# Attention and mixture of experts on one core: a table of slots for expert 0 alone, the other experts' slots by matrix products, and POOL's DMAs in the attention released a few at a time

## The chip, the cores and the metric

One Trainium2 chip, one of its cores. The metric is the device time of one execution in microseconds (us), the median over runs. Engines are named as in the profile: PE is TensorE's matmul, PEld its weight load, DVE is VectorE, ACT is ScalarE, POOL is GpSimd, SP is SyncE. POOLq and SPq are the DMAs that POOL and SP issue.

## The reference, cut to what matters

```python
# attention: 8 batches, 8 heads, 576 positions, head size 64; heads 0-3 see a plain window of 32,
# heads 4-7 a window of 128 with every fourth position
scores = np.where(masks, scale * np.matmul(q, k.transpose(0, 1, 3, 2)), -1e9)
attn = softmax(scores)
x = np.matmul(attn, v).transpose(0, 2, 1, 3).reshape(4608, 512)
# mixture of experts: 4608 tokens, 8 experts, two of them for each token
noisy_logits = x @ w_gate + np.log1p(np.exp(x @ w_noise)) * noise
top2 = np.argpartition(-noisy_logits, 2, axis=1)[:, :2]
top2_w = softmax over the two logits
for e in range(8):
    for k in range(2):
        mask = top2[:, k] == e
        h = np.maximum(x[mask] @ w1[e], 0.0)          # 512 -> 1024
        out[mask] += top2_w[mask, k, None] * (h @ w2[e])   # 1024 -> 512
```

## The kernel before, in words

**Attention.** 24 steps (`NS = 6 * U`), each of which treats 384 positions of four heads for a pair of batches. The loop is a pipeline that is written out: in turn i it emits the score products of step i (`qk`, tile `s`, line 337 and 348), the exponential of step i-1 (`expo`), its transposes (`ptr`, tile `pp`), the store and the transposes of step i-2 (`store_x`, `x_transpose`, tile `xtp`), the products with v of step i-1 (`pv`, tiles `o` and `x`, line 388) and the gate's products of step i-2 (`gate_mm`, tile `gp`, line 436). A turn has two slots; `at(kb, f)` hangs a piece of work on a slot. The results go to `xs` in HBM.

**Gate and table.** `gate(t0, n)` is a generator that works on n groups of 128 tokens in small pieces: the logits, the two best experts and their weights, and the place of each token in the list of each expert (a running count by a product with a triangle of ones, tile `posp`). `micro` lets the generators emit a few pieces at a time between the parts of a turn. Each token has two entries; an entry is a row of eight words (four row numbers of `xs`, the weight, the token's number). POOL scatters the entries into a table `tab` in HBM with an indirect DMA for each 128 tokens and each of the two experts (line 577): 72 of them. `room` limits how many of these are emitted in a slot. The table's rows beyond the entries are padding that `setup_c` writes at the start.

**Experts.** For each expert the SP queue reads its part of the table into `ixt` and `ixs` (`idx_dma`), DVE copies it into `ixi` (`idx_copy`), POOL gathers x by these numbers (`gather`, line 716, four indirect DMAs for 128 tokens; expert 0 has its own form, line 710), DVE transposes (`xsplit`, tile `xr`, line 733) and ACT and DVE split into a high and a low part (lines 735 and 736). Expert 0's transposes are PE's (`xrp`, line 730). An expert's up to 1216 tokens make up to 10 tiles in three blocks. `up` forms h for a block in eight parts of 12 products (line 764), ACT and DVE take each part out of PSUM as `hh` and `hl` (lines 768 and 769); `down` forms the output of a tile with 24 products (line 805), DVE scales it by the weight (`y`, line 814) and POOL adds it to the output's rows with an indirect DMA (line 782). The order is (up 0, down 2 of the expert before, up 1, down 0, up 2, down 1); expert 0 starts differently. First block of expert 0: its gathers and transposes fall into the attention's last turns.

**What sets the order.** After the attention `plan(t, f)` puts work into a list by the time t at which PE should be there, counted in PE's columns (`tick`); the engines execute what is emitted for them in that order, each waiting only for what an instruction needs. So a number in a `plan` call says behind which of PE's instructions something stands, not when it runs. In particular POOL had, in the attention, nothing that held its scatters back once their inputs (`si`, `en`) were there, except the scatter's own issue.

Of the kernel before, what the change touches and what calls it, by code (L numbers as in the profile page):

```python
# [9 lines left out]
F32 = mybir.dt.float32  # L10
# [11 lines left out]
T = NB * S  # L22
# [18 lines left out]
US_W2 = 3.0, 3.5  # L41
US_X = (17, 52)
# [3 lines left out]
def attention_moe_kernel(ctx, tc, qt, kp, kd, vpl, vdl, w_gate, w_noise, noise, w1, w2, out, CAPS=(1216, 1216, 1216, 1184, 1184, 1152, 1152, 1152), SPLITS=(0, 384, 896)):  # L46
# [19 lines left out]
    xq = xs.rearrange("r (q d) -> (r q) d", d=128)  # L66
    tab = dram.tile([E * ET, TC], I32, name="tab")

# [4 lines left out]
    ixp = ctx.enter_context(tc.tile_pool(name="ixp", bufs=3))  # L73
# [121 lines left out]
    i8 = gat.tile([128, NG, E], F32, name="i8")  # L195
# [5 lines left out]
    def setup_a():  # L201
# [7 lines left out]
        gpsimd.iota(i8, pattern=[[0, NG], [1, E]], base=0, channel_multiplier=0,  # L209
                    allow_small_or_imprecise_dtypes=True)  # L210
        gpsimd.iota(ebase, pattern=[[ET, E]], base=0, channel_multiplier=0,
                    allow_small_or_imprecise_dtypes=True)
        gpsimd.tensor_copy(base, ebase)
        for e in range(E):
# [4 lines left out]
    def setup_b():  # L219
# [3 lines left out]
        t = tokc[:, :, 5]  # L223
        v, s, i0, r, z, a = (acon.tile([128, 2, NT], I32, name=f"tc{i}") for i in range(6))
        gpsimd.iota(v[:, 0].rearrange("p (s j) -> p s j", j=3), pattern=[[0, 12], [128, 3]], base=0, channel_multiplier=1)
        vector.tensor_scalar(a[:, 0], t, 2, None, op0=OP.bitwise_and)
        vector.tensor_scalar(v[:, 1], t, 2, None, op0=OP.logical_shift_right)
        vector.scalar_tensor_tensor(v[:, 1], a[:, 0], 72.0, v[:, 1], op0=OP.mult, op1=OP.add)
        for u in range(U):
            c = slice(NG * u, NG * u + NG)  # L230
            gpsimd.iota(s[:, 0, c].rearrange("p (s j) -> p s j", j=3), pattern=[[768, 3], [0, 3]],
                        base=768 * (6 * u + 3), channel_multiplier=0)
            vector.tensor_scalar(a[:, 0, c], t[:, c], float(TU * u + S), 144.0, op0=OP.is_ge, op1=OP.mult)
            vector.scalar_tensor_tensor(v[:, 1, c], v[:, 1, c], -288.0 * u, a[:, 0, c], op0=OP.add, op1=OP.add)
            vector.memset(s[:, 1, c], 4608 * u)
# [61 lines left out]
    def micro(n=1):  # L297
# [4 lines left out]
        for g in list(gens):  # L302
            while n > 0 and g not in held:
# [6 lines left out]
                if r == 2:  # L310
                    room[0] -= 1
# [835 lines left out]
```

## Time and profile before

| what | us |
|---|---|
| median of 3 runs (1181.67 to 1186.98) | 1183.1 |
| profiled execution | 1184.15 |
| its span, first to last instruction | 1182.5 |
| PE busy / DVE / ACT / POOL over the span | 1026.8 / 467.6 / 298.9 / 519.9 |
| last product of the gate before the first `up` | 265.1 |
| first `up` product of expert 0 | 265.6 |

The profiled execution took 1.65 us beyond its span. The granted clock of PE was 0.941 over the span. PE carries the time: from 500 us on it is busy for 95 to 100 us of each 100, before that for 59 to 77. The stretches in which it is less busy are therefore what a change can win, and what is added to PE later on is what it can lose.

### The profile page before, as it was taken

The numbers are of one execution on the slowest core, as the hardware profiler recorded it, in microseconds if no ns is written. First come the engines' busy times: TensorE is split into PE (matmuls) and PEld (weight loads), VectorE is DVE, ScalarE is ACT, GpSimd is POOL, SyncE is SP. The second block draws the span as 40 slices with busy tenths as digits, with TensorE's granted clock in tenths as the row PEclk, the third lists the DMA queues.
The fourth block names the chain that finished last, engine by engine and source line by source line (L and its number), as shares of the span: only waits on it lengthen the run. The fifth ranks groups of instructions, "written<-read, shape, count | busy, mean of one in ns | idle before, by whom it ended". The sixth has DMA issues, their size and how long they took to land. (4 is left out here: it accounts for less than half of the span.)

```text
span 1182.5 us, 18050 instructions
## 1 busy us (share of the span) xinstructions
PE 1026.8 (87%) x7278; PEld 865.2 (73%) x7279; DVE 467.6 (40%) x1077; ACT 298.9 (25%) x540; POOL 519.9 (44%) x637
## 2 busy tenths in 40 slices
PE   5885737667589899899999998999999999999996
PEld 3663535446378787788889887978888898878885
DVE  6762524344223335243432433343434334332321
ACT  6442413342111223122222312231222223122210
POOL 5006062526456453745644562465246445624012
PEclk9997879777699999899999998999999999999998
DMA  8794538437033233352434333343424353432223
GB/s 287 266 331 182 206 126 299 150 127 271 11 62 63 70 94 94 63 115 52 118 56 108 83 89 63 81 107 74 106 47 116 68 97 91 84 94 45 54 28 45
DMA packets 70967, 133.71 MB, mean 113 GB/s; under 512 B 29520, under 2 KB 29568, under 8 KB 69600
## 3 DMA queue, kind: packets, MB, share of 16 engines
q1 hardware_dynamic: 48176, 93.22, 23.4%
q0 software_dynamic: 22704, 39.30, 18.6%
q8 instruction: 58, 0.95, 0.3%
q14 instruction: 29, 0.24, 0.1%
HBM read 92.19 MB, written 40.29 MB: 112 GB/s over the span
## 5 line engine op out<-in xcount | busy, mean ns | idle before, releaser
L764 PE MATMUL up<-x,w1h 128*128 128x512 f32 (+4 forms) x1536 | 403.4, 349 | 43.1 <-issue 16.8
L764 PEld LDWEIGHTS up<-x,w1h 128*128 128x128 f32 x1536 | 278.9, 194 | 70.3 <-DVE hl L769 18.8
L716 POOL DMA_INDIRECT g<-xs,ixi x258 | 259.7, 1007 | 107.9 <-issue 84.2
L764 PE MATMUL up<-x,w1l 128*128 128x384 f32 (+4 forms) x768 | 266.3, 347 | 1.7 <-issue 1.6
L782 POOL DMA_INDIRECT out_rows<-y,ixs x67 | 106.3, 1586 | 310.6 <-DVE y L814 260.9
L805 PE MATMUL dn<-w2h,hh 128*128 128x512 f32 x576 | 227.4, 395 | 3.3 <-issue 1.8
L805 PE MATMUL dn<-w2l,hh 128*128 128x512 f32 x576 | 226.1, 393 | 4.4 <-issue 4.4
L805 PE MATMUL dn<-w2h,hl 128*128 128x512 f32 x576 | 225.9, 392 | 3.0 <-issue 3.0
L769 DVE SCALAR_TENSOR_TENSOR hl<-up,hh 128x384 fp32r<-128x384 f32 (+2 forms) x192 | 105.7, 556 | 299.0 <-ACT hh L768 205.9
L768 ACT ACTIVATE hh<-up 128x384 fp32r<-128x384 f32 (+4 forms) x192 | 92.7, 498 | 320.7 <-PE up L764 197.0
L764 PEld LDWEIGHTS up<-x,w1l 128*128 128x128 f32 x768 | 149.1, 194 | 12.2 <-issue 1.8
L805 PEld LDWEIGHTS dn<-w2h,hl 128*128 128x128 f32 x576 | 109.3, 190 | 27.4 <-issue 4.3
L805 PEld LDWEIGHTS dn<-w2h,hh 128*128 128x128 f32 x576 | 109.5, 190 | 26.9 <-issue 4.3
L805 PEld LDWEIGHTS dn<-w2l,hh 128*128 128x128 f32 x576 | 109.5, 190 | 26.6 <-issue 4.7
L577 POOL DMA_INDIRECT tab<-en,si x72 | 70.2, 975 | 115.1 <-DVE den L397 55.5
L814 DVE TENSOR_SCALAR y<-dn,ixs 128x512 f32<-128x512 f32 x63 | 46.9, 748 | 127.8 <-PE dn L805 121.5
L735 ACT CAST x<-xr 128x512 fp32r<-128x512 f32 x67 | 40.5, 605 | 175.8 <-DVE xr L733 144.1
L649 DVE TENSOR_TENSOR w1l<-ws,w1h 128x1024 fp32r<-128x1024 f32 x32 | 38.7, 1218 | 75.3 <-ACT w1h L647 67.7
L388 PE MATMUL o<-vp,pt 128*32 128x130 f32 x576 | 32.1, 296 | 30.3 <-ACT pt L371 16.7
L710 POOL DMA_INDIRECT g<-xs,ixf x40 | 38.3, 958 | 42.8 <-DMA kt<-in_kp 21.7
L647 ACT CAST w1h<-ws 128x1024 fp32r<-128x1024 f32 x32 | 33.1, 1048 | 92.8 <-DMA ws<-in_moe_w 92.8
L733 DVE STREAM_TRANSPOSE xr<-g 128x512 f32<-128x512 f32 x67 | 45.8, 683 | 20.5 <-DMA g<-xs,ixi 16.2
(184 smaller groups left out, 839.4 us busy)
## 6 DMA issues: line engine op xcount, KB each, us to landing
ws<-in_moe_w SPq DMA_DIRECT2D x64, 512.0 KB
out_rows<-zero SPq DMA_DIRECT2D x38, 256.0 KB
vd<-in_vdl SPq DMA_DIRECT2D x24, 390.0 KB
vp<-in_vpl SPq DMA_DIRECT2D x16, 585.0 KB
xs<-x SPq DMA_DIRECT2D x24, 384.0 KB
qt<-in_qt SPq DMA_DIRECT2D x14, 576.0 KB
kt<-in_kd SPq DMA_DIRECT2D x16, 320.0 KB
g<-xs,ixi POOLq DMA_INDIRECT x258
```

Of the source, the lines that this page charges most:

```text
L577: ins = gpsimd.indirect_dma_start(out=tab, out_offset=bass.IndirectOffsetOnAxis(ap=si[:, kq, t:t + 1], axis=0), in_=en[:, kq, t], in_offse ...
L649: return lambda: vector.tensor_tensor(b, s, a.bitcast(F32), op=OP.subtract)
L710: gpsimd.indirect_dma_start(out=g[0:rn, c], out_offset=None, in_=xq[0:rows], in_offset=bass.IndirectOffsetOnAxis(ap=IX[0][0][0:rn, t, c:c ...
L716: gpsimd.indirect_dma_start(out=g[:, j], out_offset=None, in_=xq, in_offset=bass.IndirectOffsetOnAxis(ap=IX[e][1][:, r0 // 32 + j:r0 // 32 ...
L733: vector.transpose(xr[:, :, 0:rn].rearrange("p c (g t) -> p g c t", t=32), g[:, 0:n].rearrange("p g (c d) -> p g c d", d=32))
L735: scalar.copy(xh[:, :, o:o + rn], xr[:, :, 0:rn])
L764: tensor.matmul(p[:, 0:n], lhsT=a[:, 128 * f:128 * f + 128], rhs=b[:, kc, 0:n], start=(i == 0), stop=(i == 11))
L768: scalar.activation(hh[:, f, 0:n], p[:, 0:n], AF.Relu)
L769: vector.scalar_tensor_tensor(hl[:, f, 0:m], p[:, 0:m], 0.0, hh[:, f, 0:m].bitcast(F32), op0=OP.max, op1=OP.subtract)
L782: ins = gpsimd.indirect_dma_start(out=out, out_offset=bass.IndirectOffsetOnAxis(ap=sc[0:rn, t, 1:2], axis=0), in_=y[0:rn], in_offset=None, ...
L805: tensor.matmul(p[0:rn], lhsT=a[:, f, o:o + rn], rhs=b[:, f % 2], start=(i == 0), stop=(i == 23))
L814: vector.tensor_scalar(y[0:rn], p[0:rn], wsc, None, op0=OP.mult)
```

## The change

1. **Only expert 0 has a table.** A token's entry for expert 0 goes into `tab0`; a token that is not expert 0's writes into a row that nobody reads. So there is one scatter for each 128 tokens, 36 instead of 72, and the padding is a table of 10 rows a partition instead of 292.
2. **The other experts' slots come from products.** After all gates, DVE and ACT make for each of the 72 (group of 128 tokens, choice) a matrix A of ones where the slot modulo 128 matches, and a matrix V with the token's number in the column of expert and tile; PE sums A'V over all 72 into `acc` (128 x 70): the token of each slot. DVE then works out from it the output rows (`rw`), the numbers for the gathers (`xi`) and where the weight lies (`wi`). The weights are stored by token and expert in `wtab`; POOL gathers them, one indirect DMA for each tile of experts 1 to 7 (`weights`, 67 in all), after each `up` has begun. `idx_dma` and `idx_copy` for experts 1 to 7 are gone. `BULK` places the pieces: 135 of them every 0.36 us of planned time from 15 us after expert 0's start, the rest at 64 us.
3. **POOL's DMAs in the attention are released by turns.** `pool_turn` stands before each scatter and each gather of expert 0's first block. Once a turn it emits a copy of one element of `x`, the result of the latest `pv`, so that POOL waits for that step; three DMAs may follow (four from slot 40 on), each behind a memset as before.
4. **Later transposes.** `LAG`: the transposes of a gathered tile are planned 15 us behind its gather instead of 7 or 8; expert 1's gathers start at 64.1 us of expert 0 with smaller distances.
5. Smaller moves: the gates of groups 18 to 23 and 24 to 26 are one of nine groups at slot 43; the token numbers are worked out by a generator instead of at once.

```diff
-    def new_slot(scatters, speed=1):
-        room[0], rate[0] = scatters, speed
+    def new_slot(scatters, speed=1):
+        if scatters:
+            room[0], fresh[0] = scatters, True
+        rate[0] = speed
         held.clear()
+    def pool_turn():
+        while room[0] <= 0:
+            yield 1
+        if fresh[0] and not experts[0]:
+            gpsimd.tensor_copy(spacer, late["x"])
+        else:
+            gpsimd.memset(spacer, 0.0)
+        fresh[0] = False
+        room[0] -= 1
...
-        new_slot(*((3, 1) if kb < 28 else (4, 2)))
+        new_slot((0 if kb % 2 else 3 if kb < 40 else 4), 1 if kb < 28 else 2)
...
         for t in range(n):
-            for kq in range(2):
-                gpsimd.memset(spacer, 0.0)
-                ins = gpsimd.indirect_dma_start(
-                    out=tab, out_offset=bass.IndirectOffsetOnAxis(ap=si[:, kq, t:t + 1], axis=0),
-                    in_=en[:, kq, t], in_offset=None)
+            yield from pool_turn()
+            ins = gpsimd.indirect_dma_start(
+                out=tab0, out_offset=bass.IndirectOffsetOnAxis(ap=si[:, t:t + 1], axis=0),
+                in_=en[:, t], in_offset=None)
...
+    def slots():
...
+        for i in range(m + 3):
+            if i < m:
+                if i % 4 == 0:
+                    av = late["stage"].tile([128, 4, 256], F32R, name="av", tag="ws")
+                A, V = av[:, i % 4, 0:128], av[:, i % 4, 128:128 + NO]
+                if i % 2:
+                    vector.tensor_scalar(A, iof, lo[:, i:i + 1], None, op0=OP.is_equal)
+                else:
+                    scalar.activation(A, iof, AF.Abs, bias=nlo[:, i:i + 1])
+                    scalar.activation(A, A.bitcast(F32), AF.Relu, scale=-1.0, bias=one)
+                vector.tensor_scalar(V, iof[:, 0:NO], d[:, i:i + 1], tokf[:, i // 2:i // 2 + 1],
+                                     op0=OP.is_equal, op1=OP.mult)
+                ops[i] = (A, V)
+            if i >= 3:
+                A, V = ops.pop(i - 3)
+                tensor.matmul(acc, lhsT=A, rhs=V, start=(i == 3), stop=(i == m + 2), skip_group_check=True)
+            yield
...
+    def weights(e, t):
+        c, rn = NC * (e - 1) + t, TLS[e][t][1]
+        gpsimd.indirect_dma_start(out=late["wq"][0:rn, c:c + 1], out_offset=None, in_=wtab,
+                                  in_offset=bass.IndirectOffsetOnAxis(ap=late["wi"][0:rn, c:c + 1], axis=0))
...
+    def first_block():
+        for t in range(BLS[0][0][0], BLS[0][0][1]):
+            for c in range(4):
+                yield from pool_turn()
+                gather(0, t, (c,))
+                yield 0
...
+            bulk = others()
+            for i in range(135):
+                plan(start + BULK[0] + BULK[1] * i, lambda: next(bulk, None))
+            plan(start + BULK[2], lambda: [None for _ in bulk])
             experts[0] = True
         else:
-            plan_x(e, 2, start + 2, 7, 8)
+            plan_x(e, 2, start + 2, 7, LAG)
         if not last:
-            t = start + (42 if first else 20)
-            plan(t, lambda e=e: (new_idx(e + 1), idx_dma(e + 1, 0, CAPS[e + 1])))
-            plan(t + 8, lambda e=e: idx_copy(e + 1, 0, CAPS[e + 1]))
-            t = max(t + 9, at_[0, 1])
-            plan_x(e + 1, 0, t, 7, 8)
-            plan_x(e + 1, 1, t + 21, 8, 8)
+            t = max(start + (BULK[2] + 0.1 if first else 29), at_[0, 1])
+            plan_x(e + 1, 0, t, *((5, 10) if first else (7, LAG)))
+            plan_x(e + 1, 1, t + (15 if first else 21), *((5, 12) if first else (7, LAG)))
...
+                if e:
+                    for i, ti in enumerate(range(BLS[e][bi][0], BLS[e][bi][1])):
+                        plan(now[0] + 1 + 1.5 * i, lambda ti=ti, e=e: weights(e, ti))
                 up((e, bi), X.pop((e, bi)), BLS[e][bi][3], tail(e, bi))
```

Three places show how the instructions stand. First POOL in the attention, where the scatters of the first gate begin. `tab` is the table of all experts, `spacer` a tile of one element, `en` and `si` a group's entries and their places. Before:

```order
L281 MEMSET free 128x784
L576 MEMSET spacer 1x1
L577 DMA tab<-en,si 37376x8
L576 MEMSET spacer 1x1
L577 DMA tab<-en,si 37376x8
```

And after, where `tab_58` is the table of expert 0 and `x` the result of the latest step:

```order
L246 IOTA tokc 128x36
L343 COPY spacer<-x 1x1
L640 DMA tab_58<-en,si 9216x8
L345 MEMSET spacer 1x1
L640 DMA tab_58<-en,si 9216x8
L345 MEMSET spacer 1x1
L640 DMA tab_58<-en,si 9216x8
L343 COPY spacer<-x 1x1
L640 DMA tab_58<-en,si 9216x8
```

Before, the pair of memset and scatter repeats 36 times (two gates) with nothing of the attention in between; now each three scatters stand behind a copy from a step's `x`. In the whole attention there are 13 such groups: six of three scatters, the gathers of expert 0's first block as groups of 3, 4, 4 and 1, and the third gate's scatters as 4, 4 and 1. Behind them stand 16 gathers and nine scatters without copies; before, that last stretch was 16 gathers and 12 scatters, and six more scatters later.

The second place is PE at the beginning of expert 0's second `up` (tiles `w1h`, `w1l`: the high and low part of w1; `x`: the split tokens). Before:

```order
L805 MATMUL dn<-w2h_3556,hl 128x512
L764 MATMUL up<-x,w1h_2842 128x512 x2
L764 MATMUL up<-x,w1l_2843 128x512
L764 MATMUL up<-x,w1h_2904 128x512 x2
L764 MATMUL up<-x,w1l_2905 128x512
L764 MATMUL up<-x,w1h_3100 128x512 x2
L764 MATMUL up<-x,w1l_3101 128x512
L764 MATMUL up<-x,w1h_3142 128x512 x2
L764 MATMUL up<-x,w1l_3143 128x512
```

And after, with `acc` the sum over all tokens and `av` the pairs of A and V:

```order
L987 MATMUL dn<-w2h_3487,hl 128x512
L946 MATMUL up<-x,w1h_2715 128x512 x2
L946 MATMUL up<-x,w1l_2716 128x512
L946 MATMUL up<-x,w1h_2791 128x512 x2
L946 MATMUL up<-x,w1l_2792 128x512
L946 MATMUL up<-x,w1h_3029 128x512 x2
L946 MATMUL up<-x,w1l_3030 128x512
L946 MATMUL up<-x,w1h_3058 128x512 x2
L946 MATMUL up<-x,w1l_3059 128x512
L755 MATMUL acc<-av 128x70 x7
```

Behind each of the eight parts of that `up` there now stand seven to nine products into `acc`; the other 12 of the 72 stand in the `down` ahead of it.

The third place is POOL in the middle experts (`ixi`, and `xi` after, hold the numbers for the gathers; `out_rows` is the output). Before:

```order
L782 DMA out_rows<-y,ixs 4864x512
L716 DMA g<-xs,ixi 128x128 x9
L781 MEMSET spacer 1x1
L782 DMA out_rows<-y,ixs 4864x512
L781 MEMSET spacer 1x1
```

And after, with `wq` the weights of the slots:

```order
L964 DMA out_rows<-y,rw 4864x512
L900 DMA wq<-wtab,wi 128x1
L894 DMA g<-xs,xi 128x128 x4
L900 DMA wq<-wtab,wi 128x1 x2
L894 DMA g<-xs,xi 128x128 x5
L963 MEMSET spacer 1x1
L964 DMA out_rows<-y,rw 4864x512
```

The gathers and the output's DMAs are as many as before; nine or ten gathers of weights for each expert stand among them, and no read of a table on SP or DVE is left there.

More of the change, by code (lines that the diff above doesn't have):

```diff
@@ L1004, in attention_moe_kernel, with others @@
             plan(2.0 * (kb - NK - 5), f)
+    def others():
+        while not ready[0]:
+            yield
+        late["en"] = gat.tile([128, 2, 2 * NT], F32, name="lg", bufs=2)
+        late["en2"] = gat.tile([128, 2 * NT], F32, name="lg", bufs=2)
+        yield from slots()
     start = 0.0
```

429 lines of the change are left out of this document (295 added, 134 removed).

## The prediction

> **What bounds the kernel now.** I read the page's slices first, then windows of whole steps, then the two timelines of PE and POOL where a window was poor, and last the windows and rows behind the attention. The slices (29.6 us each) show PE short of work in the first ten and nearly full from the eighteenth on:
>
> ```profile
> PE   5885737667589899899999998999999999999996
> PEclk9997879777699999899999998999999999999998
> ```
>
> The program is thus two parts: an attention that PE could do faster and experts that PE bounds. A step of the attention begins with the same product each time, and these rows give its length when nothing disturbs it:
>
> ```profile
> 45.92 0.50 PE L337 MATMUL s<-mask,identb 128*128 128x512 bf16 x2
> 78.68 0.50 PE L337 MATMUL s<-mask,identb 128*128 128x512 bf16 x2
> ```
>
> Five steps lie between them: (78.68 - 45.92) / 5 = 6.55 us. Cutting at the same product, I find four single steps of four times that length or a little less. The windows below hold those five good steps together, the four long ones, the step behind the first of these, and the stretches up to and behind the attention's end at 265.6 (columns: length, busy time and instructions of PE, PEld, DVE, ACT and POOL, granted clock, DMA share, GB/s):
>
> ```profile
> 45.92:78.68 32.76, 29.26 (x643) 24.12 (x640) 20.19 (x53) 17.04 (x38) 1.07 (x3) 1.00 0.93 352
> 94.44:122.40 27.96, 12.55 (x132) 6.58 (x130) 3.95 (x12) 3.21 (x6) 18.97 (x36) 0.67 0.31 107
> 122.40:131.38 8.98, 8.36 (x131) 6.70 (x130) 3.69 (x9) 3.21 (x6) 0.00 (x0) 0.71 0.72 252
> 153.11:181.89 28.78, 9.70 (x130) 6.97 (x127) 3.94 (x12) 3.75 (x9) 18.75 (x35) 0.65 0.26 91
> 195.24:210.59 15.35, 8.69 (x140) 6.12 (x137) 7.72 (x41) 3.81 (x10) 7.73 (x9) 0.85 1.02 408
> 217.44:243.00 25.56, 12.94 (x136) 6.97 (x131) 7.08 (x30) 6.36 (x15) 16.72 (x28) 0.75 0.25 80
> 265.60:283.00 17.40, 17.34 (x91) 16.86 (x90) 11.25 (x55) 4.52 (x10) 9.64 (x11) 0.85 0.65 217
> 283.00:312.60 29.60, 8.61 (x22) 5.78 (x21) 1.18 (x10) 1.43 (x2) 20.43 (x34) 0.58 0.43 146
> ```
>
> In each long step PE has its usual 130 to 140 instructions, while POOL works nearly without pause. What POOL does there is indirect DMAs back to back: 18 scatters in the first and in the second, 8 gathers in the third, and 12 scatters with 4 gathers in the fourth, 60 in all; 28 more follow at 273.2. First and last of the first burst, a group of six later that stands by itself, and the burst of 28:
>
> ```profile
> 96.30 1.09 POOL L577 DMA_INDIRECT tab<-en,si  x1 [33.63 <-DVE si L572]
> 117.97 0.96 POOL L577 DMA_INDIRECT tab<-en,si  x1 [0.23 <-issue]
> 259.90 0.96 POOL L577 DMA_INDIRECT tab<-en,si  x1 [20.66 <-DVE den L397]
> 266.87 0.96 POOL L577 DMA_INDIRECT tab<-en,si  x1 [0.23 <-issue]
> 273.22 0.98 POOL L710 DMA_INDIRECT g<-xs,ixf  x1 [5.39 <-issue]
> 307.47 0.96 POOL L577 DMA_INDIRECT tab<-en,si  x1 [0.22 <-issue]
> ```
>
> The period is (117.97 - 96.30) / 17 = 1.27 us a DMA, and its last ends at 118.93, 3.5 us before the step does. The mechanism that I read: while POOL issues these, PE's instructions are let through only slowly.
>
> ```profile
> 106.00:122.00 16.00, 4.80 (x16) 1.78 (x17) 0.00 (x0) 0.00 (x0) 10.80 (x22) 0.50 0.03 3
> 112.16 0.37 PE L436 MATMUL gp<-xt,wg 128*32 128x128 f32 x1 [0.85 <-issue]
> 113.57 0.44 PE L436 MATMUL gp<-xt,wg 128*32 128x128 f32 x2 [1.04 <-issue]
> ```
>
> Two products start in 1.41 us, so one instruction per 0.70 us (matmuls or weight loads), each with idle time put to "issue", that is to no semaphore. The DMA share of 0.03 says that the transfers are not what is full. But it doesn't begin at once. From a burst's first DMA until PE falls to that pace, PE still works through some 100 instructions:
>
> ```profile
> 96.30:100.82 4.52, 3.33 (x52) 2.64 (x49) 2.18 (x3) 1.72 (x3) 3.87 (x7) 1.00 0.73 244
> 153.82:157.40 3.58, 2.86 (x59) 2.12 (x47) 0.91 (x2) 1.41 (x4) 3.14 (x6) 1.00 0.97 360
> 198.04:202.96 4.92, 2.58 (x49) 1.96 (x47) 4.43 (x30) 2.11 (x5) 3.85 (x4) 1.00 1.01 409
> 218.91:225.25 6.34, 3.20 (x59) 2.52 (x48) 4.07 (x9) 3.31 (x4) 5.14 (x8) 1.00 0.41 147
> ```
>
> So PE has a store of about 100 instructions (96 to 107), good for 3.6 to 6.3 us, in the mean 4.8; a burst that ends before it is used up should cost nothing.
>
> **The change part by part.** *Pacing and 36 scatters fewer.* The four steps are 27.96 + 28.78 + 15.35 + 25.56 = 97.65 us; four good ones are 26.2, so 71.4 us are lost in them, and another 2.4 in the step of 8.98 us behind the first, which runs at a clock of 0.71. With 13 groups of one to four DMAs, one behind each step's `x`, I let all of it go: -73.8.
>
> *What the groups still cost.* Three DMAs last 3.8 us and four 5.1. Against the mean store of 4.8 us the seven groups of three cost nothing and the four groups of four run over by 0.3 us; once starved, PE recovered late (3.5 us above). From below: 0, since the six scatters from 259.90 on, 7.9 us, left PE busy in 265.60:283.00 for 17.34 of 17.40 us. From above, with the shortest store of 3.6 us and 3.5 us of recovery each: 7 x (3.8 + 3.5 - 3.6) + 4 x (5.1 + 3.5 - 3.6) = 46. I take 2 us for each group of four: +8, near the low end, as three of the four stores seen outlast a group of three.
>
> Each copy waits for `pv` of its turn, and behind it on POOL are only the next scatters and gathers. Of the attention nobody waits for a scatter; expert 0's gathers and the first `up` wait for the table, and their groups are last. The first scatter ran at 96.30, in the thirteenth of 24 steps; with the two turns that drain the pipeline 14 turns are left for the 13 groups, so this just fits, and what is late is within the bounds of the term behind the attention.
>
> *Transfers.* The attention without stalls is denser. A row for its queue up to 265.6:
>
> ```profile
> q1 hardware_dynamic: 15414, 56.70, 58.9%
> ```
>
> 58.9% of 265.6 is 156 us, so an attention of 200 us has a share of 0.78, and the good steps above ran at 0.93. Contention: 0 to 5, I take +2. The padding's smaller writes and the moved gate of nine groups are in there; the smaller work for `en` on DVE is hidden beside a PE that is busy for 29.26 of 32.76 us.
>
> By the Trainium skill (DMA: Bandwidth & Descriptors, "Issuing engines are not separate DMA queues") DMAs of all issuing engines share the same 16 engines, and spreading them saves only the sequencer's time. Were the stalls such a sharing, spreading would return nothing and the sum would be 1184 + 10 + 1 = 1195; the share of 0.03 inside the stall speaks against it, so I keep the 71.4.
>
> *Behind the attention.* In 283.00:312.60 PE is idle for 21 us under the burst of 28 DMAs. After the change 16 gathers and nine scatters stand there with no copies: three DMAs fewer, 3 x 1.27 = 3.8, so -4. Ends: -21 if it goes altogether, and +12 if the burst comes so early that it meets the attention's short products, where the store lasts 4.8 us and not the 17.4 that expert 0's long products gave it.
>
> *The slots by products.* New on PE are 72 products into 128x70, on DVE 36 A and 72 V, on ACT 72 operations, all in expert 0. The nearest rows:
>
> ```profile
> 317.98 0.66 PE L730 MATMUL xrp<-ident,g 128*128 128x128 f32 x4
> 318.40 0.48 PE L805 MATMUL dn<-w2h,hh 128*128 128x512 f32 x1
> 88.40 0.39 PE L540 MATMUL posp<-ob,ones 128*128 128x72 bf16 x9
> L526 DVE TENSOR_TENSOR oh<-i,xf 128x72 f32<-128x72 f32 x4 | 0.8, 229 | 0.1
> L769 DVE SCALAR_TENSOR_TENSOR hl<-up,hh 128x512 fp32r<-128x512 f32 x64 | 43.8, 690 | 93.5 <-ACT hh L768 78.9 <-issue 8.7 <-ACT w2h L660 5.9
> ```
>
> Four transposes take 0.42 us until the next product, 0.105 each: 72 x 0.105 = 7.6 us. The bf16 products of 72 columns take 0.043 each, or 3.1. I take the first, as these are 32 bit wide too, and 2 us for DVE: its 108 operations are 108 x 0.229 = 25 us, among `hl` that PE waits for, but `hl` itself stands idle for twice its busy time. +10, from 3 to 20 (7.6 and half of DVE's 25).
>
> *The experts.* Gone are the table's reads and the copies to `ixi`. 67 weight gathers come, at 1.27 us each 85 us of POOL, 12 per expert.
>
> ```profile
> 900.00:1000.00 100.00, 97.40 (x497) 85.10 (x496) 39.32 (x61) 24.66 (x42) 48.18 (x50) 1.00 0.39 85
> L716 POOL DMA_INDIRECT g<-xs,ixi x258 | 259.7, 1007 | 107.9 <-issue 84.2
> 392.43 0.44 ACT L768 ACTIVATE hh<-up 128x320 fp32r<-128x320 f32 x1 [6.61 <-remote]
> 393.60 0.67 PE L764 MATMUL up<-x,w1h 128*128 128x320 f32 x2 [4.85 <-issue]
> 607.14 0.38 PE L764 MATMUL up<-x,w1h 128*128 128x320 f32 x1 [2.31 <-DVE hh L772]
> 1037.54 0.51 PE L764 MATMUL up<-x,w1h 128*128 128x256 f32 x2 [2.03 <-DVE hl L769]
> ```
>
> POOL is half busy there, so it has the room; PE's long products make its store last. But PE does stop at the third `up` of experts, six times from 605 to 1038 (first and last quoted), 15.1 us in all, at the ends of POOL's bursts. There the weight gathers lengthen the burst by three or four DMAs: +4 of my choosing. The later transposes (`LAG`) take DVE's work out of such a burst: -3 from stops like that of 4.85. Together +1, from -15 (the six stops go) to +20 (one more us at each of the 21 `up`s of experts 1 to 7).
>
> Sum: 1184.15 - 71.4 - 2.4 + 8 + 2 - 4 + 10 + 1 = 1127.4 us. The execution profiled is 1.05 us above the median of 1183.1, so 1126 as a median.
>
> **The rivals.** *Stalls by the DMA.* The loss may go with each DMA and not with a store's end: 71.4 / 60 = 1.19 us each. The attention's 39 would cost 46 us, which gives 1127.4 - 8 + 46 = 1165. For it: three of the stores are within 1.3 us of a group's length. Against it: the six scatters at 259.90.
>
> *Faster.* The burst behind the attention and the six stops go as well: -17 more for the first, -15 for the second, 1127.4 - 32 = 1095. For it: later transposes and a POOL that is early. Against: 25 of the 28 DMAs are still unheld.
>
> *Slower.* POOL's bursts in experts 1 to 7 now hold the weights too; if each of the 21 `up`s stops as at 393.60 but for three more DMAs (3.5 us), that is 21 x 3.5 = 74, so 1201. It would decide from (1184 - 1127) / 21 = 2.7 us on each. Against it: 97.40 of 100 us busy in 900:1000 with POOL's present load.
>
> *Not paced.* The copies may read an `x` that is long done, POOL runs late and catches up: bursts of 36 + 12 DMAs without pause, at 1.19 each 57 us kept, 1176.
>
> **How the numbers follow.** The forecast has 0.64, stalls by the DMA 0.16, faster 0.10, slower 0.05, not paced 0.03; 0.02 goes to the spreading that returns nothing (1195). By its terms' bounds the forecast's own range is 1100 to 1150. The range reaches to the rivals at 1095 and 1165 with a little beside them, 1092 to 1170. A measurement here can tell about 0.5%, 5.9 us. Only the slower rival and the sharing end above 1189; a part of not paced and of the upper tails is within 0.5%: faster 0.89, same 0.04, slower 0.07.
>
> **What the changed profile would show.** The first product of the steps should come every 6.5 to 8 us with no step above 12, the attention's end near 200 us; POOL's copies should each have an idle time ended by DVE's or ACT's `x`, with three or four DMAs behind. If PE has "issue" idle times of 0.7 us behind each third DMA, the stalls go by the DMA. Behind the attention a hole of about 17 us should remain under the unheld burst. The `acc` products should add 7 to 8 us of PE time in expert 0's first 70 us or so. In experts 1 to 7 PE should stay 95 us busy of each 100; stops of over 3 us at every `up` with POOL's weight gathers just before would make it slower. The forecast fails most likely in the store: if it is shorter when the DMA share is high (153.82:157.40 has the shortest, at 0.97), each group of three costs too.

## The result, and the profile after

The changed kernel takes 1241.3 us (median of 4 runs, 1224.5 to 1246.4), the kernel before 1185.0 in the same comparison (1181.7 to 1188.3): 1.043 times as long, interval 1.036 to 1.049. Forecast were 1126 us and a gain. Ratios and intervals here and below are taken over the runs within 1.5% of the fastest of the same kernel, medians in us over all runs. The profiled execution has a span of 1240.4 us. Its slices of 31 us, from the page of the changed kernel:

```profile
PE   6887776767978858799899998997999798889995
PEclk9999988878998979899889999998999999989998
```

The attention is denser than before, but from the 18th slice on, in the experts, sevens and eights stand where nearly all slices had nines. Whole stretches of the changed kernel, in the columns of the prediction's windows (length, busy us and instructions of PE, PEld, DVE, ACT, POOL, clock, DMA share, GB/s); the first two are pairs of steps with nine scatters each, the third is the end of the attention, the fourth expert 1's first two `up`s, the last what follows them:

```profile
97.30:118.60 21.30, 14.79 (x262) 10.83 (x260) 7.95 (x22) 6.35 (x12) 9.84 (x18) 0.92 0.85 297
140.30:162.70 22.40, 16.16 (x259) 12.60 (x255) 7.42 (x20) 6.69 (x15) 9.68 (x18) 0.85 0.87 289
203.20:231.00 27.80, 18.81 (x245) 14.05 (x241) 11.18 (x35) 9.38 (x19) 11.05 (x18) 0.75 0.47 150
402.62:465.19 62.57, 44.19 (x193) 36.32 (x192) 24.45 (x37) 16.84 (x28) 29.77 (x33) 0.86 0.25 66
465.19:1240.40 775.21, 702.03 (x3401) 601.55 (x3399) 261.66 (x418) 155.90 (x262) 380.67 (x405) 0.96 0.33 72
```

The kernel before, in the stretch that answers to the last row (from the first `down` behind expert 1's first two `up`s):

```profile
463.26:1182.50 719.24, 688.73 (x3401) 596.45 (x3399) 263.82 (x438) 155.07 (x262) 331.52 (x354) 0.98 0.37 79
```

PE has the same 3401 products in both. So the time divides like this:

| stretch | before | after | difference |
|---|---|---|---|
| start to the first `up` | 265.6 | 231.0 | -34.6 |
| from there to the first `down` behind expert 1's first two `up`s | 197.6 | 234.2 | +36.6 |
| the rest: experts 1 to 7 | 719.2 | 775.2 | +56.0 |
| span | 1182.5 | 1240.4 | +57.9 |

In the rest, PE idles for 73.2 us (775.21 - 702.03) where it idled for 30.5, and its products are 13.3 us longer at a clock of 0.96 instead of 0.98. New there are the weight gathers (page, group of line 900):

```profile
L900 POOL DMA_INDIRECT wq<-wtab,wi x67 | 67.3, 1004 | 20.4 <-issue 18.0 <-DMA g<-xs,xi 2.4
```

One stop as the timelines show it. POOL issues 18 DMAs without a pause under the third block's `up` of an expert, three of them weights, from 831.2 to 855.7; the first row is the window, the others are ACT's and PE's first instructions after the stop:

```profile
831.20:855.70 24.50, 17.71 (x112) 16.11 (x110) 5.71 (x14) 2.79 (x6) 19.47 (x21) 0.99 0.27 54
856.66 0.41 ACT L950 ACTIVATE hh<-up 128x288 fp32r<-128x288 f32 x1 [6.94 <-remote]
857.77 0.82 PE L946 MATMUL up<-x,w1h 128*128 128x288 f32 x2 [6.45 <-DVE hh L954]
```

ACT does not take `up` out of PSUM for 6.9 us and goes on 1 us after POOL's last DMA; PE, with no free `up` tile, waits for it. As in the attention an engine stands still while POOL issues, ACT this time. Where the 56 us lie can be read from the same timelines: 28.6 of them in the seven third `up`s with the `down`s behind them (312.3 us against 283.7), the rest at other places, such as 8.8 in the second `up` at 1025.7 (30.6, where the kernel before has 21.8).

### The profile page after: what moved, and what is told of

Read it like the earlier page. It is cut to its first block, busy times and chain, and to the rows that moved or that the text cites. A ratio compares the mean times of both kernels' runs of the same rounds, so it can differ in the third digit from the quotient of the medians.

```text
span 1240.4 us, 18405 instructions
## 1 busy us (share of the span) xinstructions
PE 1052.1 (85%) x7349; PEld 883.7 (71%) x7350; DVE 502.4 (41%) x1219; ACT 325.1 (26%) x609; POOL 546.6 (44%) x640
## 5 line engine op out<-in xcount | busy, mean ns | idle before, releaser
L946 PE MATMUL up<-x,w1h 128*128 128x512 f32 (+4 forms) x1536 | 410.5, 353 | 67.9 <-DVE hh L954 29.5
L946 PEld LDWEIGHTS up<-x,w1h 128*128 128x128 f32 x1536 | 282.5, 197 | 96.3 <-DVE hl L951 26.7
L894 POOL DMA_INDIRECT g<-xs,xi x258 | 252.2, 977 | 78.6 <-issue 77.4
L946 PE MATMUL up<-x,w1l 128*128 128x384 f32 (+4 forms) x768 | 269.6, 351 | 4.0 <-issue 4.0
L964 POOL DMA_INDIRECT out_rows<-y,rw x67 | 108.1, 1614 | 322.5 <-DVE y L996 303.1
L987 PEld LDWEIGHTS dn<-w2h,hl 128*128 128x128 f32 x576 | 110.1, 191 | 28.6 <-issue 5.4
L996 DVE TENSOR_SCALAR y<-dn,wq 128x512 f32<-128x512 f32 x63 | 46.8, 746 | 111.5 <-PE dn L987 89.0
L900 POOL DMA_INDIRECT wq<-wtab,wi x67 | 67.3, 1004 | 20.4 <-issue 18.0
L918 DVE TENSOR_TENSOR x<-xr,x 128x512 fp32r<-128x512 f32 x67 | 44.7, 666 | 18.7 <-ACT x L917 17.9
```

Source lines behind the costliest of these rows:

```text
L894: gpsimd.indirect_dma_start(out=g[:, j], out_offset=None, in_=xq, in_offset=bass.IndirectOffsetOnAxis(ap=ix, axis=0))
L900: gpsimd.indirect_dma_start(out=late["wq"][0:rn, c:c + 1], out_offset=None, in_=wtab, in_offset=bass.IndirectOffsetOnAxis(ap=late["wi"][0: ...
L918: return lambda: vector.tensor_tensor(xl[:, :, o:o + rn], xr[:, :, 0:rn], xh[:, :, o:o + rn].bitcast(F32), op=OP.subtract)
L946: tensor.matmul(p[:, 0:n], lhsT=a[:, 128 * f:128 * f + 128], rhs=b[:, kc, 0:n], start=(i == 0), stop=(i == 11))
L964: ins = gpsimd.indirect_dma_start(out=out, out_offset=bass.IndirectOffsetOnAxis(ap=row_, axis=0), in_=y[0:rn], in_offset=None, compute_op= ...
L987: tensor.matmul(p[0:rn], lhsT=a[:, f, o:o + rn], rhs=b[:, f % 2], start=(i == 0), stop=(i == 23))
```

## The experiments

Every time is compared with the kernel before, run beside it on the same chip. The groups of trials fell on different chips (numbers 2, 1, 14 and 6), on which the kernel before took 1203, 1185, 1202 and 1055 us; this turned out to be the main finding and is taken up last. Runs on these chips, the last excepted, scatter by 1 to 3%, so differences under 1% between two trials are not read. The changed kernel itself was run again on chips 1 and 6, not on 2 and 14.

**Chip 2: which part of the change.** Theory W: the weight gathers. Theory L: the later transposes.

*no_weights* removes the calls of `weights` and sets `wq` to 0.5 once.

```diff
-                if e:
-                    for i, ti in enumerate(range(BLS[e][bi][0], BLS[e][bi][1])):
-                        plan(now[0] + 1 + 1.5 * i, lambda ti=ti, e=e: weights(e, ti))
```

> The changed kernel without the 67 weight gathers of experts 1 to 7 (a constant 0.5 stands for the weights); all else as it is. Theory W, the weight gathers lengthen POOL's bursts and ACT and DVE are held at the third block's up until a burst ends: the 56 us by which experts 1 to 7 became longer mostly go, 1241 - 45 = about 1195. Theory L, the later transposes (LAG 15) run into hh and hl: the gathers are innocent, 1231 to 1241.

Measured: 1204.9 us against 1203.4, ratio 1.000 (0.995 to 1.004). The whole loss is gone, as theory W has it, and nothing of the forecast gain has come in its place. From the trace, the stretch of experts 1 to 7:

```profile
457.62:1194.60 736.98, 694.94 (x3401) 601.68 (x3399) 261.01 (x418) 155.18 (x262) 321.27 (x345) 0.97 0.36 76
```

PE idles for 42.0 us there, where it idled for 73.2 in the changed kernel.

*lag8* has `LAG = 8`.

> The changed kernel with LAG 8 instead of 15, the weight gathers kept. Theory W: the time stays within about 8 us of the changed kernel, 1233 to 1249. Theory L: the 56 us of experts 1 to 7 mostly go, about 1195.

Measured: 1283.7 us, ratio 1.066 (1.058 to 1.075). Theory L is refuted in its direction: going back costs. How much is the lag's own is less clear, since *no_pace* (LAG 15) took 1273.5 and *quiet_weights* (LAG 15) 1253.1 on the same chip.

*no_pace* replaces the copy from `x` by a memset.

```diff
-        if fresh[0] and not experts[0]:
-            gpsimd.tensor_copy(spacer, late["x"])
-        else:
-            gpsimd.memset(spacer, 0.0)
+        gpsimd.memset(spacer, 0.0)
```

> The changed kernel with each copy from x on POOL made a memset, so that POOL's DMAs in the attention are no longer held to a step; order and number unchanged. If a burst's cost begins only when PE's store of instructions is used up (the prediction), bursts of 18, 18 and 12 come back and the attention ends some 20 to 30 us later: 1260 to 1270. If each DMA costs the same wherever it stands (the rival of the stalls by the DMA), nothing changes: 1236 to 1246.

Measured: 1273.5 us, ratio 1.059 (1.051 to 1.067). By the ratio this lies between the two expectations (1236 to 1246 and 1260 to 1270 are 1.043 to 1.051 and 1.063 to 1.072 of 1185). The bursts that came back were of nine and not of 18, as there is one scatter for each 128 tokens now. The attention ended at 246.5 us here; with the copies, on the same chip, it ended at 246.0 in *quiet_weights*, 246.5 in *lag8* and 236.1 in *no_weights*, so its end alone tells nothing clear. The pairs of steps with nine scatters, in one unbroken burst of nine (first two rows, *no_pace*) and as six and three (last two, *quiet_weights*; the second copy of a gate finds its `x` done and doesn't hold POOL back, so two groups of three become one of six, in the changed kernel's own profile too):

```profile
99.42:123.56 24.14, 16.86 (x263) 11.94 (x259) 7.96 (x22) 6.36 (x12) 9.55 (x18) 0.79 0.66 227
145.28:170.59 25.31, 13.32 (x260) 10.90 (x256) 7.47 (x21) 6.71 (x15) 9.42 (x18) 0.80 0.63 206
```

```profile
99.37:123.07 23.70, 16.12 (x262) 12.36 (x259) 8.19 (x24) 6.34 (x12) 9.83 (x18) 0.86 0.79 274
144.96:168.35 23.39, 17.70 (x258) 12.52 (x255) 7.47 (x21) 6.66 (x15) 9.69 (x18) 0.78 0.88 295
```

Two good steps are 13.1 us, so nine scatters cost 11.0 and 12.2 us unbroken and 10.6 and 10.3 us in groups: 1.2 to 1.4 and 1.1 to 1.2 a DMA. Pacing of this kind gave a tenth, not all. Where the rest of the 1.6% between this trial's ratio and the changed kernel's lies, in code that is the same, is not settled.

*quiet_weights* plans the weight gathers of expert e + 1 from the second `down` of expert e on, one every 2.1 us.

> The changed kernel with each expert's weight gathers moved to the second down of the expert before (one every 2.1 us), where POOL issues only single output DMAs; as many of them. Theory W by the length of the bursts: most of the 56 us go, 1195 to 1210. If each weight gather costs wherever it stands: 1236 to 1246. Theory L: 1236 to 1246 too.

Measured: 1253.1 us, ratio 1.040 (1.030 to 1.050): no better. But the trace shows that the place was badly chosen: POOL runs late, three of each expert's ten weights still stood at the end of the burst under the third `up`, and that burst had 18 DMAs as in most experts of the changed kernel.

**Chip 1: where the gathers stand.** *after_again* is the changed kernel.

> The changed kernel again, as the control on the chip of the other three. All theories: 4 to 5% over the kernel before on this chip.

Measured: 1246.3 us (1219.3 to 1252.2) against 1185.3. The four runs lie too far apart for an interval, but the loss is there again.

*quiet2* begins the weights 8 us later than *quiet_weights*.

> The changed kernel with each expert's weight gathers from 8 us after the start of the second down of the expert before, one every 2.1 us: behind the last gathers of x, and no longer three of them in the burst that lies under the third block's up, as in the first such trial. If only the length of that burst counts: 25 to 40 us below the changed kernel on the same chip. If each weight gather costs about 0.75 us wherever it stands (51 us for 67): within 8 us of it.

Measured: 1231.1 us, ratio 1.039 (1.031 to 1.047), 15 us below the changed kernel's median on this chip. The bursts under the third `up` had 15 DMAs again, and from expert 2 on that `up` took 15 to 19 us in the trace where it took 20 to 23 in *quiet_weights*; but the weights that moved now made the bursts at the experts' start longer, and the stops came there (20.5 to 21.7 us for a `down` that takes 14.6 in the kernel before). Neither expectation holds fully: the length of a burst counts where an engine runs dry in it, and none of the places tried was free of both.

*early* is *quiet2* with the gathers of x from 22 us into an expert on, 6 us apart (the lines on the weights are left out):

```diff
-            t = max(start + (BULK[2] + 0.1 if first else 29), at_[0, 1])
-            plan_x(e + 1, 0, t, *((5, 10) if first else (7, LAG)))
-            plan_x(e + 1, 1, t + (15 if first else 21), *((5, 12) if first else (7, LAG)))
+            t = start + BULK[2] + 0.1 if first else start + 22
+            plan_x(e + 1, 0, t, *((5, 10) if first else (6, LAG)))
+            plan_x(e + 1, 1, t + (15 if first else 18), *((5, 12) if first else (6, LAG)))
...
```

> As the one before, and the gathers of x for the next expert begin 22 us into an expert instead of some 31, 6 us apart instead of 7, so that POOL's last burst ends before or early in the third block's up. If that up's wait for ACT while the burst lasts is what the experts lose: another 10 to 25 us less, at or below the kernel before. If the gathers cost wherever they stand: the same as the one before; if the output's DMAs now wait behind more gathers: slower than it.

Measured: 1217.0 us, ratio 1.022 (1.011 to 1.033): 14 us below *quiet2*, but not at or below the kernel before. The third `up` of one expert and the `down` behind it, in the changed kernel (first pair) and here (second pair), from PE's timelines:

```profile
837.29 0.42 PE L946 MATMUL up<-x,w1h 128*128 128x288 f32 x2
860.79 0.63 PE L987 MATMUL dn<-w2h,hh 128*128 128x512 f32 x1
```

```profile
828.54 0.42 PE L946 MATMUL up<-x,w1h 128*128 128x288 f32 x2
841.18 0.39 PE L987 MATMUL dn<-w2h,hh 128*128 128x512 f32 x1
```

23.5 us have become 12.6: the stop at the burst's end goes if the burst ends earlier. The burst that has moved, 27 DMAs from 782.5 to 820.1 us, lies under an `up` of 21.8 us and a `down` of 16.3, as long as in the kernel before, so a DMA does not cost the same everywhere. The stretch of experts 1 to 7 takes 737.8 us here, as little as without the weights; what stays lost lies ahead of them, from expert 0's first `up` on (235.1 us where the kernel before takes 197.6).

*before_lag15* is the kernel before with transposes 15 us behind their gathers.

> The kernel before with transposes 15 us behind each gather instead of 8; nothing else. The changed kernel lost 28 us by going back to 8, with POOL busier. If that is the delay of transposes that wait for a late gather and hold hl on DVE behind them, the kernel before gains a part of it: 1 to 15 us less. If it needs POOL's weight gathers: no change, within 5 us.

Measured: 1187.7 us, ratio 1.004 (1.000 to 1.008): the lag alone gives nothing.

**Chip 14: the suspected cost by itself.** *before_plus67* adds to the kernel before, at the same planned places, 67 gathers that nobody reads (the lines that define `x1` and plan the calls are left out):

```diff
+    def extra(e, t):
+        c, (r0, rn) = (10 * (e - 1) + t) % 64, TLS[e][t]
+        gpsimd.indirect_dma_start(out=tri.bitcast(F32)[0:rn, c:c + 1], out_offset=None, in_=x1,
+                                  in_offset=bass.IndirectOffsetOnAxis(ap=IX[e][1][0:rn, r0 // 32:r0 // 32 + 1], axis=0))
...
```

> The kernel before with the changed kernel's 67 small gathers (128 rows of 4 bytes, read by nobody) planned at the same places, one to four behind the start of each up of experts 1 to 7; nothing else. If they alone cost what their removal from the changed kernel gave back (51 us): 1185 + 35 to 55 on a chip that gives 1185. If they cost only beside the changed kernel's later transposes and late first gathers: up to 15 us.

Measured: 1266.3 us against 1202.1, ratio 1.056 (1.050 to 1.062), 64 us or 0.96 us a gather of 128 numbers of 4 bytes. Theory W holds without the rest of the change.

*double_scatter* puts a second scatter, into a table that is not read, behind each of the attention's 27.

> The changed kernel with each of the 27 scatters of the attention's gates followed by a second one into a table that nobody reads: groups of three become six, of four eight. If a DMA costs the attention about its own 1.2 us wherever it stands: 27 x 1.2 = 32 us later, the attention's end included. If a group costs only beyond PE's store of 4.8 us, as the prediction had it: the groups of three (3.8 us) begin to stall, 7 x (7.6 + 3.5 - 4.8) and 2 x (10.1 + 3.5 - 4.8), 62 us.

Measured: 1299.2 us, ratio 1.082 (1.073 to 1.090). The two pairs of steps, now with 18 scatters each in groups of twelve and six:

```profile
91.74:127.78 36.04, 19.63 (x261) 12.89 (x259) 8.18 (x23) 6.34 (x12) 19.24 (x36) 0.76 0.53 182
149.51:185.89 36.38, 19.03 (x258) 12.93 (x256) 7.65 (x22) 6.68 (x15) 19.05 (x36) 0.72 0.58 198
```

Less 13.1, they cost 22.9 and 23.3 us, 1.3 a DMA; the kernel before paid 1.2 a DMA for 18 in one step. For nine to 18 in two steps the price is thus between 0.9 a DMA (8.2 us for nine in 97.30:118.60 above) and 1.4. The attention's end says the same: it is at 267.3 us here and at 228.5 in *pause* and 237.9 in *best1*, which have the same attention without the second scatters on the same chip. That is 29 to 39 us for 27 DMAs, where the two expectations were 32 and 62: the cost goes by the DMA.

*pause* lets POOL rest for some 2.4 us (12 small memsets) before every fifth gather of experts 1 to 7, in the changed kernel.

> The changed kernel with a rest of some 2.4 us (12 small memsets of POOL) before every fifth gather of experts 1 to 7, weights included: 65 rests, 156 us of POOL. If ACT and PE are held by the length in which POOL issues without a break: the stops at the third up shrink, 15 to 40 us less than the changed kernel. If they are held by each DMA: no change within 8 us. If POOL then only ends its bursts later: slower by 5 to 40 us.

Measured: 1230.5 us, ratio 1.027 (1.020 to 1.033), below the changed kernel's 1.036 to 1.049 (measured on another chip). But the trace does not show the gain where the rests were meant to give it:

```profile
445.40:1224.90 779.50, 702.56 (x3401) 605.09 (x3399) 263.91 (x421) 155.44 (x264) 530.83 (x1093) 0.95 0.34 73
```

Experts 1 to 7 take 779.5 us where the changed kernel took 775.2; the stop moves from the third `up` to the `down` behind it, which lasts 28 to 32 us instead of 22. What is shorter is the stretch ahead, from expert 0's first `up` on (216.9 us against 234.2). The row shows one thing more: POOL is busy for 150 us longer than in the changed kernel (530.8 against 380.7) and the stretch is 4 us longer, across two chips. So POOL's time by itself costs little on a chip with stalls.

*best1* is *early* with the weights of expert 1 from 7 us into it, its third block's gathers 17 us and the next expert's 30 us into it, and the later experts' weights from 3 us into the second `down`, 1.9 us apart.

> As the trial with early gathers, and the weight gathers of expert 1 begin 7 us into it, its third block's gathers 17 us and the next expert's 30 us into it; in the later experts the weight gathers begin 3 us into the second down, 1.9 us apart, so that they end before the next gathers. If the first up of expert 1 lost its 20 us by the burst of 29 DMAs under it: 10 to 20 us below the trial with early gathers, 0.5 to 1.5% above the kernel before. If what is lost there is the late start of its gathers behind the products: no change.

Measured: 1226.8 us, ratio 1.010 (1.004 to 1.015). Its ten runs spread from 1207.0 to 1243.3 us, and their median is 1.020 times that of the kernel before, so whether it beats *early* is not shown. Neither is below the kernel before.

**Chip 6.** Three trials were to tell whether a gather costs by POOL's time or as a DMA, what expert 1's late start costs, and whether tighter gathers help the kernel before. *before_rest67* replaces the extra gather by `for _ in range(4): gpsimd.memset(tri, 0.0)`.

> The kernel before with 67 times four memsets on POOL (128x128 bf16, some 1.1 us for the four) where the trial with 67 small gathers had a gather each: POOL's time without the DMAs. If the gathers cost by delaying what stands behind them on POOL: about as slow as that trial, +40 to +64 us. If they cost because PE and ACT are held while POOL issues a DMA: 0 to 12 us.

Measured: 1065.3 us against 1055.2, ratio 1.010 (1.008 to 1.013).

*before_late1* plans expert 1's gathers as the changed kernel does.

> The kernel before with expert 1's gathers planned as in the changed kernel (from 64.1 us of expert 0 instead of 51, 5 us apart, the second block 15 us later); nothing else. If their late start is what makes expert 1's first ups longer: +8 to +18 us. If that came from the weight gathers in the same burst alone: within 4 us.

Measured: 1056.4 us, ratio 1.001 (0.999 to 1.003).

*before_early* has gathers 5 us apart and transposes 15 us behind them, from expert 3's on.

> The kernel before with the gathers of the next expert 5 us apart instead of 7 or 8, the second block 15 us behind the first instead of 21, transposes 15 us behind the gathers, from expert 3's on. If the end of POOL's last burst sets the third up's stop (2.2 to 3.6 us each, five of them): 5 to 15 us less. If the burst only becomes denser: within 4 us, or up to 10 us slower.

Measured: 1056.0 us, ratio 1.001 (0.999 to 1.002). None of the three says what it was made for, because on this chip there is nothing to disturb. The kernel before took 1055 us. Here are three steps of its attention, unchanged in *before_late1*, under the same unbroken burst of 18 scatters (96.5 to 119), and the stretch of experts 1 to 7:

```profile
94.59:114.41 19.82, 17.81 (x391) 14.77 (x388) 11.30 (x28) 9.46 (x18) 14.86 (x29) 1.00 0.92 329
364.30:1052.10 687.80, 677.22 (x3401) 588.40 (x3399) 265.49 (x438) 155.61 (x262) 332.64 (x353) 1.00 0.40 82
```

6.61 us a step, with POOL issuing all the time. Three of the kernels were run again, and these runs fell on chip 6 too.

*after_third*:

> The changed kernel. On a chip whose kernel before takes about 1190 us: +4 to +5% as twice before. On one whose kernel before takes about 1055 us, without the stalls: the attention gains nothing, the products and expert 1's late start still cost, the weight gathers little: +5 to +25 us.

Measured: 1070.7 us against 1055.6, ratio 1.014 (1.011 to 1.016).

*plus67_again*:

> The kernel before with the 67 small gathers. On a chip with stalls: +50 to +65 us again. On one without: 0 to 12 us, like the memsets there.

Measured: 1063.9 us, ratio 1.007 (1.004 to 1.010).

*rest67_again*:

> The kernel before with 67 times four memsets instead of those gathers. On a chip with stalls: +40 to +64 us if it is POOL's time, 0 to 15 us if it is the DMAs. On one without: +11 us as just measured.

Measured: 1064.6 us, ratio 1.009 (1.007 to 1.012). On chip 6 the 67 gathers cost what 67 pieces of POOL's time cost, 8 to 10 us; on chip 14 they cost 64. The stretch of experts 1 to 7 of the kernel with the gathers, on chip 14 and on chip 6:

```profile
471.77:1258.50 786.73, 711.15 (x3401) 610.05 (x3399) 264.52 (x438) 153.46 (x262) 388.10 (x414) 0.95 0.35 72
```

```profile
371.55:1064.60 693.05, 679.95 (x3401) 589.63 (x3399) 266.15 (x438) 154.41 (x262) 394.56 (x414) 1.00 0.40 82
```

POOL does the same work in both (388 and 395 us); PE idles for 75.6 us in the one and for 13.1 in the other. The burst of 18 DMAs that is shown above for the changed kernel, in the same expert on chip 6:

```profile
702.40:726.80 24.40, 24.40 (x149) 22.35 (x148) 10.34 (x25) 6.29 (x13) 19.33 (x21) 1.00 0.30 56
```

As long on POOL (24.4 against 24.5 us, 19.3 against 19.5 busy), and PE loses nothing. These memsets were not run on a chip with stalls; *pause*, on chip 14, is the nearest to it. What stays open is what on chips 1, 2 and 14 lets an indirect DMA's issue hold PE, ACT and DVE, and whether it is the chip or something else that differed between these groups of runs.

## Why the prediction was wrong, step by step

The terms of the sum beside what the profile of the changed kernel shows, in us:

| part | forecast | measured |
|---|---|---|
| attention (-71.4, -2.4, +8, +2) | -63.8 | -34.6 |
| expert 0 and expert 1's first two `up`s (-4, +10) | +6 | +36.6 |
| the rest: experts 1 to 7 | +1 | +56.0 |

- **The good step, the stalls and their cause.** Right on chips like the profiled one: POOL's bursts held PE, and the DMA share was not what was full; on chip 6 these steps are 6.6 us long.
- **The store of 100 instructions.** This step failed, and with it the term "let all of it go: -73.8" with +8 for the groups. With nothing for the groups the sum has the attention's end at 265.6 - 73.8 = 191.8; it was at 231.0. Some 11 of these 39 us are not held time at all: on chip 6, without stalls, the same attention ends at 202.7. The other 28 are, 0.7 for each of 39 DMAs, and other profiles of the same attention end between 228.5 and 246.5. A group of three costs by itself, as the second steps of the two pairs above show, which have three scatters each and are 6.61 and 6.84 us long on chip 6:

```profile
108.72:118.57 9.85, 7.14 (x130) 5.54 (x130) 3.40 (x7) 3.10 (x6) 3.25 (x6) 0.88 0.78 273
151.30:162.74 11.44, 9.13 (x132) 7.49 (x130) 3.72 (x10) 3.12 (x6) 3.22 (x6) 0.70 0.87 292
```

That is 3.2 and 4.6 us, 1.1 and 1.5 a DMA, where the prediction had nothing. It shows why the store does not help: it is PE's, and ACT and DVE are held too. In the first of these steps PE had ended `s` at 111.7 and `pp` at 112.5, and POOL's last DMA ended at 113.6. Only after that DVE takes `s` and ACT takes `pp`, 6.0 and 6.1 us into the step, and PE then waits for ACT. On chip 6 (last two rows, step from 107.09) they take them 2.1 and 2.8 us into it:

```profile
114.68 0.96 DVE L403 TENSOR_REDUCE mx<-s 128x12 f32<-128x768 f32 x1 [4.96 <-PE xtp L465]
114.81 0.80 ACT L421 COPY pt<-pp 128x768 f32<-128x768 f32 x1 [4.53 <-PE xtp L465]
116.04 0.55 PE L465 MATMUL xtp<-ident,x 128*128 128x128 f32 x3 [2.70 <-ACT xt L467]
109.17 0.96 DVE L403 TENSOR_REDUCE mx<-s 128x12 f32<-128x768 f32 x1 [0.75 <-PE s L398]
109.93 0.80 ACT L421 COPY pt<-pp 128x768 f32<-128x768 f32 x1 [1.23 <-PE pp L418]
```

The rival of the stalls by the DMA had it: 46 us for 39 DMAs. 21 DMAs fewer at 1.2 us are 25 of the 34.6 us gained; the other 10 are no more than what profiles of one attention differ by. The rival of copies that find their `x` done came true in part, with the groups of six.

- **The row of six scatters at 259.90**, taken as evidence against that rival, was misread: its window begins at 265.60, behind four of the six. Where they lie, PE was busy for 2.5 of 5.7 us:

```profile
259.90:265.60 5.70, 2.53 (x28) 1.84 (x29) 2.31 (x4) 1.87 (x6) 4.84 (x8) 0.87 0.62 186
```

And in 265.60:283.00 PE had 91 long products, which need few instructions.

- **The weights: +4.** This is the largest error; without the weights the ratio is 1.000. The term priced POOL's time ("it has the room") and not the hold. The price was in the sum's own first term: 71.4 us for 60 DMAs, which makes 80 for 67. The addition to the kernel before gave 64 us (0.96 each); the removal 4.3% or 51 us (0.76 each), across two chips. The slower rival had the size, 2.7 us on each of 21 `up`s; measured were 56 us, 2.7 each on the mean, but half of it at the third `up`s and the `down`s behind them and not at each `up`. That the mean fits is in part luck. Its 0.05 was too little, since "97.40 of 100 us busy" shows an average at POOL's present load and not what three more DMAs at the end of a burst of 15 do.
- **Expert 0: +10 and -4.** Measured +36.6. The two terms themselves were near: the first `up` and the `down` behind it took 58.6 us where they took 66.2 (-7.6 for the -4), and the second `up`, with the products, 42.7 where it took 28.7 (+14.0 for the +10; 12.8 us of PE busy by the page against 7.6, and 9.8 us of waiting for DVE and ACT against 2). What failed is that the rest was put at nothing: the third `up` and `down` took 52.7 us where they took 40.8, and expert 1's first two `up`s 62.6 where they took 44.5. Under the former lie 20 gathers of expert 1 in one burst of 22 DMAs (350.0 to 378.6), under the latter, from 411 to 442, 25 DMAs without a pause, gathers and the first weights. Without the weights the latter took 48.7. That expert 1's gathers move behind the products stands in the change and had no term in the sum; *before_late1*, made to price it, fell on chip 6, so its share on a chip with stalls is not shown.

```profile
L755 PE MATMUL acc<-av 128*128 128x70 f32 x72 | 12.8, 280 | 9.8 <-DVE av L750 6.3 <-ACT av L749 1.7 <-ACT av L748 1.0
```

- **The spreading that returns nothing.** By the Trainium skill (DMA: Bandwidth & Descriptors, "Issuing engines are not separate DMA queues") DMAs of several issuing engines run on the same 16 engines, and issuing from several saves only the sequencer's time. That page of the Trainium skill does not speak of one engine's DMAs released in groups; that this returns nothing, and the 1195, were the prediction's own reading. It came nearer to the result than the sum, by luck: pacing did return little, but the DMA share within stalls is low (0.03) and chip 6 issues the same DMAs without a stall.
- **Chips.** The sum rests on one profile of one chip. With the hold absent the change costs 15 us (1.014). There the attention has no stalls to give back; the gathers alone, added to the kernel before, cost 7 to 8 us.

## What to carry to other kernels

Price an indirect DMA of POOL by what the other engines lose beside it, not by POOL's idle time: divide a stall in the trace by the DMAs in it and charge that to every DMA that a change adds, however few bytes it has, until a trace shows a place where it costs less. Grouping such DMAs gave a tenth here where it could be compared; having fewer of them, or placing them so that a burst ends under long products, gave more. And before tuning against a stall, look whether a second chip shows it at all.

## What the runs showed of the hardware

The kernel before took 1183 to 1203 us on all chips but one, and 1055 on chip 6, where the granted clock over the span was 0.98 instead of 0.94. In the kernel before it was 0.50 in the stall of 106.00:122.00 and 1.00 in the undisturbed steps, so the lower mean goes with the stalls; which of the two causes the other is not shown. POOL's own pace is the same on both kinds; its scatters in the profile of before and in *before_late1*:

```profile
L577 POOL DMA_INDIRECT tab<-en,si x72 | 70.2, 975 | 115.1 <-DVE den L397 55.5 <-DVE si L572 44.6 <-issue 15.0
```

```profile
L577 POOL DMA_INDIRECT tab<-en,si x72 | 70.1, 974 | 65.5 <-DVE si L572 35.6 <-issue 14.9 <-DVE den L397 14.8
```

The rows of a gather hardly matter to POOL: in the changed kernel one of 128 rows takes mostly 0.94 us, one of 64 rows 0.91 (second of these) and one of 32 rows 0.88 (third):

```profile
487.06 0.94 POOL L900 DMA_INDIRECT wq<-wtab,wi  x1 [0.30 <-DMA g<-xs,xi]
488.31 0.91 POOL L900 DMA_INDIRECT wq<-wtab,wi  x1 [0.30 <-issue]
...
735.93 0.88 POOL L900 DMA_INDIRECT wq<-wtab,wi  x1 [0.31 <-issue]
```

Which engine is held in a burst differs by what runs: PE in a long burst among short products, ACT and DVE in a group of three there, ACT with `hh` where PE's products are long.
